# Attention and GELU MLP on one core: first batch's exps ahead of AV, gated loads, regrouped filler, q and k transposed in the idle score banks

## Chip, cores, metric

The kernel runs on one core of a Trainium2 chip. The time is the device time of one execution in microseconds (us), taken as the median of several runs; the span that the profile shows for the same execution is about 2 us shorter. Numbers that are read from a trace belong to one profiled execution.

## The reference

For 8 batches of 8 heads with 576 tokens of 64 elements, a causal attention with a decay from forget gates f, then a two-layer MLP with exact GELU over all 4608 tokens:

```python
scores = scale * np.matmul(q, k.transpose(0, 1, 3, 2))
cum    = np.cumsum(np.log(np.clip(f, 1e-4, 1.0)), axis=-1)
scores = np.where(causal, -1e9, scores + cum[..., :, None] - cum[..., None, :])
# ... softmax over the last axis ...
x = (attn @ v).transpose(0, 2, 1, 3).reshape(B * S, H * D)     # 4608 x 512
h = x @ w_in                                                   # 512 -> 2048
out = (0.5 * h * (1 + erf(h / np.sqrt(2)))) @ w_out            # 2048 -> 512
```

The decay's part in k goes into v as a weight per token (the weights wT, from f), the part in q cancels in the softmax.

## The kernel before

The program is a hand-ordered stream. For each batch: 16 score tiles (4 pairs of heads, 4 tiles each), the exps on ScalarE (ACT), causal masks on GpSimd (POOL), then AV (the product of the exps with the weighed v), the normalization and an output transpose. Then 16 blocks of GEMM1 with GELU. The 64 GEMM2 matmuls of batch b-1 are not run by themselves: they are filler, taken a few at a time between the score tiles of batch b. The 96-token transposes of the next batch's q and k stand between the GEMM1 blocks.

```python
    s_psum = ctx.enter_context(tc.tile_pool(name="s_psum", bufs=2, space=PSUM))  # scores
    o_psum = ctx.enter_context(tc.tile_pool(name="o_psum", bufs=2, space=PSUM))  # AV, transposes
    m_psum = ctx.enter_context(tc.tile_pool(name="m_psum", bufs=2, space=PSUM))  # GEMMs
# ... all loads are issued at once, in this order:
    # f; q, k of batch 0; v of batch 0; w_in; q, k, v of batch 1; w_out
# ...
    def transposes(b, i, which):            # one tensor (q or k) of one pair
        ps = o_psum.tile([P, 2, JT // 2, PT], BF16, tag="o", name="ps_t")
        # ... 6 transposes of 128 columns, then four VectorE copies of 64x288 ...
# ...
    for i in range(HP):                     # batch 0: everything transposed first
        transposes(0, i, 0)
        transposes(0, i, 1)
    # ... the weights wT ...
    for i in range(HP):
        weigh_v(0, i)                       # on GpSimd
    for b in range(B):
        # ... load_qk(b + 2), load_v(b + 2) ...
        for i in range(HP):
            for t in range(4):
                scores(b, i, t)             # exp and masks within
                # ... half a head of AV of pair i-1, normalize, to_xT ...
                take(fill, 2)               # two GEMM2 matmuls of batch b-1
        # ... take 4, AV, take 4, AV, take 8, to_xT ...
        for ffb in range(n_ff):
            gemm1(b, ffb)
            if b + 1 < B:
                if ffb % 2 == 1:
                    transposes(b + 1, ffb // 4, (ffb // 2) % 2)
                if ffb % 4 == 2:
                    weigh_v(b + 1, ffb // 4)
```

The softmax here doesn't subtract the row's maximum and nothing guards it: scores larger than these inputs give would overflow.

## Time and profile before

| | before |
|---|---|
| median of 3 runs | 420.17 us (418.93 to 422.03) |
| span of the profiled execution | 419.1 us |
| TensorE busy | 88% |
| first exp / first GEMM1 matmul | 23.7 / 57.8 us |
| batch 0's GEMM1, to the first score of batch 1 | 57.84 to 75.90: 18.1 us |
| period of a batch afterwards | 43.0, then 42.72 |

TensorE is the engine to feed. The list of waits (who waited for whom: total us, times, longest) of TensorE names what starves it; its first rows, and one further down:

```profile
PE s L210 <- ACT e L220: 10.3, 11, 1.2
PE o L241 <- POOL e L222: 9.7, 13, 7.2
...
PE o L241 <- POOL vw L201: 7.0, 1, 7.0
```

The last two belong to the start-up: one wait of 7.2 us for a mask and one of 7.0 us for the weighed v. The first is spread over the batches: 11 waits of at most 1.2 us in which a score tile waits for an exp to free its bank. The prediction below shows the other lines.

### The profile page before, as it was taken

How to read it: one execution, taken by the hardware profiler on the slowest of the kernel's cores; microseconds unless marked ns; L12 is line 12 of the kernel's file. 1: busy time of each engine (PE TensorE's matmuls, PEld its weight loads, DVE VectorE, ACT ScalarE, POOL GpSimd, SP SyncE). 2: the span in 40 equal slices, each digit the busy share in tenths (PEclk: the TensorE clock that was granted, in tenths of full speed). 3: DMA queues.
4: the chain of work that ended last, by engine and by line, in shares of the span. 5: the costliest groups of instructions: out<-in, count | busy, mean ns of one | idle time of the engine just before them, and what ended most of it. 6: DMA issues, size and time to landing. Idle time of an engine off the chain costs nothing.

```text
span 419.1 us, 7515 instructions
## 1 busy us (share of the span) xinstructions
PE 368.4 (88%) x3045; PEld 207.5 (50%) x3045; DVE 207.2 (49%) x466; ACT 215.0 (51%) x291; POOL 129.5 (31%) x262
## 2 busy tenths in 40 slices
PE   1340879899989998999899989998999999999996
PEld 1220645465546554655465546654664456444442
DVE  6930339534954486448634773468355924102001
ACT  3040736872677267725773577447743675350620
POOL 8408460446034603460247024700470042000000
PEclk9999969999999999999999999999999999999999
DMA  9999985801671166216521643100001000102002
GB/s 156 209 193 196 193 186 125 114 28 54 148 109 31 51 152 93 48 51 152 82 58 52 152 65 74 46 31 2 27 27 51 2 25 28 50 0 77 25 25 77
DMA packets 62738, 34.19 MB, mean 82 GB/s; under 512 B 43184, under 2 KB 57520, under 8 KB 62704
## 3 DMA queue, kind: packets, MB, share of 16 engines
q0 software_dynamic: 15328, 13.63, 20.9%
q1 hardware_dynamic: 47376, 20.08, 18.7%
q8 instruction: 24, 0.39, 0.4%
q14 instruction: 10, 0.08, 0.1%
HBM read 37.90 MB, written 9.44 MB: 113 GB/s over the span
## 4 chain that ended last, share of the span: by engine, by line
PE 77%; ACT 8%; POOL 5%; issue 4%; DVE 4%; ACTq 0%; POOLq 0%
PE ps L277 30%; PE ps L297 26%; PE s L210 7%; PE o L241 7%; ACT e L220 6%; PE ps_t L170 4%; POOL e L222 3%; PE ps_x L265 2%; DVE kT L181 2%; ACT L220 1%; DVE qB L181 1%; DVE qA L181 1%; POOL vw L195 1%; POOL q L98 1%; POOL k L98 1%
## 5 line engine op out<-in xcount | busy, mean ns | idle before, releaser
L289 ACT ACTIVATE g<-ps 128x512 bf16<-128x512 f32 x144 | 86.0, 597 | 125.7 <-PE ps L277 125.7
L297 PE MATMUL ps<-w_out_sb,g 128*128 128x512 bf16 x576 | 146.2, 379 | 0.0
L277 PE MATMUL ps<-xT_sb,w_in_sb 128*128 128x512 bf16 x576 | 136.5, 383 | 0.0
L220 ACT ACTIVATE e<-s 128x1024 bf16<-128x1024 f32 (+2 forms) x128 | 105.7, 862 | 56.2 <-PE s L210 47.6
L222 POOL TENSOR_SCALAR_AFFINE_SELECT e<-e 128x256 bf16<-128x256 bf16 x160 | 62.5, 406 | 114.7 <-ACT e L220 114.3
L277 PEld LDWEIGHTS <-w_in_sb 128*128 128x128 bf16 x576 | 54.0, 99 | 58.2 <-issue 3.5
L241 PE MATMUL o<-vw,e 128*128 128x65 bf16 x960 | 53.9, 196 | 17.7 <-POOL e L222 9.7
L297 PEld LDWEIGHTS <-g 128*128 128x128 bf16 x576 | 49.4, 98 | 37.8
L254 DVE RECIPROCAL r<-o 128x5 f32<-128x5 f32 x64 | 12.5, 195 | 110.5 <-PE o L241 110.5
L210 PE MATMUL s<-qA,kT 128*128 128x384 bf16 (+2 forms) x192 | 54.6, 289 | 11.3 <-ACT e L220 10.3
L181 DVE COPY kT<-ps_t 64x288 bf16<-64x288 bf16 x128 | 61.3, 479 | 2.5 <-PE ps_t L170 0.3
L306 DVE COPY ot<-ps 128x512 f32<-128x512 f32 x36 | 24.7, 687 | 75.7 <-PE ps L297 75.7
L210 PEld LDWEIGHTS <-kT 128*128 128x128 bf16 x384 | 37.2, 100 | 47.1 <-issue 17.2
L241 PEld LDWEIGHTS <-e 128*128 128x128 bf16 x960 | 45.5, 99 | 29.7 <-POOL e L222 11.3
L210 PE MATMUL s<-qB,kT 128*128 128x384 bf16 (+2 forms) x192 | 49.7, 290 | 0.0
L195 POOL TENSOR_TENSOR vw<-v,wT 128x640 bf16<-128x640 f32 x32 | 40.8, 1276 | 15.9 <-issue 13.1
L181 DVE COPY qA<-ps_t 64x288 bf16<-64x288 bf16 x64 | 30.6, 478 | 13.7 <-PE ps_t L170 12.5
L98 POOL DMA_DIRECT2D q<-in_q_dram x11 | 8.4, 766 | 80.3 <-PE ps_t L170 78.7
L255 DVE TENSOR_TENSOR x<-o,r 128x320 bf16<-128x320 f32 x64 | 31.4, 491 | 2.2
L181 DVE COPY qB<-ps_t 64x288 bf16<-64x288 bf16 x64 | 30.7, 480 | 0.9
L170 PE MATMUL ps_t<-ident_bf,q 96*128 96x96 bf16 x192 | 14.6, 216 | 11.6 <-POOL ident_bf masks.py:199 7.2
L170 PEld LDWEIGHTS <-q 96*128 96x128 bf16 x192 | 12.4, 103 | 18.9 <-issue 7.0
(33 smaller groups left out, 117.2 us busy)
## 6 DMA issues: line engine op xcount, KB each, us to landing
out_dram<-ot SPq DMA_DIRECT2D x36, 256.0 KB, 2.0
v<-in_v_dram SPq DMA_DIRECT2D x64, 128.0 KB, 3.1
q<-in_q_dram POOLq DMA_DIRECT2D x7, 576.0 KB, 6.0
k<-in_k_dram POOLq DMA_DIRECT2D x7, 576.0 KB, 8.0
w_in_sb<-in_moe_w_in_dram POOLq DMA_DIRECT2D x4, 512.0 KB, 12.1
v<-in_v_dram SPq DMA_DIRECT2D x8, 256.0 KB, 3.4
w_out_sb<-in_moe_w_out_dram POOLq DMA_DIRECT2D x4, 512.0 KB, 25.7
q<-in_q_dram POOLq DMA_DIRECT2D x4, 144.0 KB, 6.2
```

Of the source, the lines that this page charges most:

```text
L170: nc.tensor.transpose(ps[:, h, j, :], src[:, 2 * i + h, 2 * j * D : 2 * (j + 1) * D], ident_bf[:PT, :PT],)
L181: nc.vector.tensor_copy(rows[:, odd], ps[odd * D : (odd + 1) * D, h].rearrange("d j p -> d p j"),)
L195: nc.gpsimd.tensor_tensor(vw_of[b][:, hs, :, 0:D], v_of[b][:, hs, :, :], w.unsqueeze(3).to_broadcast([P, 2, NBLK, D]), Alu.mult,)
L210: nc.tensor.matmul(st[:, h, c : c + w], kT[i][:, K0[n] : K0[n] + P], qt[:, q0 : q0 + w], start=True, stop=True,)
L220: nc.scalar.activation(et[:, :, 0:c], st[:, :, 0:c], Act.Exp, scale=scale)
L222: nc.gpsimd.affine_select(out=et[:, :, c0 : c0 + P], in_=et[:, :, c0 : c0 + P], compare_op=Alu.is_ge, fill=0.0, base=0, pattern=[[0, 2], [ ...
L241: nc.tensor.matmul(o[:, m, :], e_of[b, i, t][:, h, c : c + P], vw_of[b][:, 2 * i + h, n, :], start=(n == 0), stop=(n == m),)
L255: nc.vector.tensor_tensor(x_of[b, i][:, :, h, :], o[:, :, 0:D], r.unsqueeze(2).to_broadcast([P, NBLK, D]), Alu.mult,)
L277: nc.tensor.matmul(ps, w_in_sb[:, kt, ffb * P : (ffb + 1) * P], xT_sb[:, kt, t0 : t0 + TC], start=(kt == 0), stop=(kt == n_dm - 1),)
L289: nc.scalar.activation(g_of[c][ffb], ps, Act.Gelu)
L297: nc.tensor.matmul(ps, g_of[c][kt][:, ts * P : (ts + 1) * P], w_out_sb[:, kt, :], start=(kt == 0), stop=(kt == n_ff - 1),)
L306: nc.vector.tensor_copy(ot, ps)
```

## The change

It has five parts.

1. *Load order.* q and k of batch 0 come in three portions. A GpSimd memset in v's tile holds v's loads back until q and k of four heads are issued (the "gate"). w_in comes in four column blocks, issued after the second pair's v is weighed; q, k of batch 1 and w_out only after batch 0's last exps are issued. q, k and v have one buffer each instead of two.
2. *Batch 0's transposes* write 64 rows each, so that one evacuation (the copy out of the bank) takes a whole tensor (kT) or half of one (qA, qB); two are on ACT.
3. *Batch 0's order.* Scores and exps begin after pair 0's transposes, and run two pairs ahead of AV; the tiles of exps have three buffers instead of two.
4. *Filler.* The GEMM2 matmuls are no longer two per tile: twelve follow the second score tile of a batch, and AV is put after the second to fourth tile. Batch 1 gets almost none before its last pair, because w_out comes late.
5. *Transposes of later batches* go into a score bank, q and k of a pair together, one group each four blocks; the eight copies follow. For batch 1 only three groups stand there, after blocks 8, 12 and 15; the fourth goes through the output banks within batch 1's own attention.

```diff
-    for i in range(HP):
-        load_qk(0, 2 * i, 2 * i + 2)
-    load_v(0)
+    load_qk_tokens(0, 0, 2)
     ... identities ...
+    load_qk_tokens(0, 2, 4)
+    v_of[0] = v_pool.tile([P, H, NBLK, D], FP32, tag="v", name="v0")
+    nc.gpsimd.memset(v_of[0][:, :, 0, 0:1], 0.0)
+    load_v(0, 0, 4)
+    load_qk_tokens(0, 4, 8)
+    load_v(0, 4, 8)
     ...
+    def transposes_pe(b, i, in_s=True):
+        if in_s:
+            both = s_psum.tile([P, 2, 2 * 512], BF16, tag="s", name="s_t")
+        ... both tensors' 12 transposes, then eight VectorE copies ...
     ...
+    def first_attention():
+        transposes(0); scores(0, 0, 0); scores(0, 0, 1)
+        ... wT; transposes(1); scores(0, 0, 2..3); transposes(2) ...
+        weigh_v(0, 0, nc.vector)
+        weigh_v(0, 1)
+        ... load_w_in(0..3); scores(0, 1, 0..3); transposes(3) ...
+        weigh_v(0, 2, nc.vector)
+        scores(0, 2, 0); scores(0, 2, 1)
+        attend_pair(0, 0)
+        ... and so on, two pairs ahead of AV ...
+    FILL = [[0, 12, 4, 4], [2, 3, 3, 2], [2, 3, 3, 2], [2, 2, 2, 2], [8, 4, 4, 0]]
+    FILL_1 = [[0, 0, 0, 0], [0, 0, 0, 0], [0, 0, 0, 0], [0, 0, 2, 4], [8, 4, 4, 0]]
     ...
-                take(fill, 2)
+                take(fill, counts[i][t])
     ...
-                if ffb % 2 == 1:
-                    transposes(b + 1, ffb // 4, (ffb // 2) % 2)
+                at = (8, 12, 15) if b == 0 else (1, 5, 9, 13)
+                if ffb in at:
+                    transposes_pe(b + 1, at.index(ffb))
```

(Several statements are put on one line here; the rest of the diff is the same code moved.)

More of the change, by code (lines that the diff above doesn't have):

```diff
@@ L75 @@
     consts = ctx.enter_context(tc.tile_pool(name="consts", bufs=1))
-    qk_pool = ctx.enter_context(tc.tile_pool(name="qk", bufs=2))
-    v_pool = ctx.enter_context(tc.tile_pool(name="v", bufs=2))
-    e_pool = ctx.enter_context(tc.tile_pool(name="e", bufs=2))
+    qk_pool = ctx.enter_context(tc.tile_pool(name="qk", bufs=1))
+    v_pool = ctx.enter_context(tc.tile_pool(name="v", bufs=1))
+    e_pool = ctx.enter_context(tc.tile_pool(name="e", bufs=3))
     x_pool = ctx.enter_context(tc.tile_pool(name="x", bufs=3))
@@ L87, with load_qk_tokens @@
     qk_of, v_of = {}, {}
-    def load_qk(b, h0=0, h1=H):
-        if b >= B:
-            return
+    def load_qk_tokens(b, h0=0, h1=H):
         if b not in qk_of:
-            qk_of[b] = (
-                qk_pool.tile([PT, H, JT * D], BF16, tag="q", name=f"q{b}"),
-                qk_pool.tile([PT, H, JT * D], BF16, tag="k", name=f"k{b}"),
-            )
+            qk_of[b] = [
+                qk_pool.tile([PT, H, JT * D], BF16, tag=n, name=f"{n}{b}")
+                for n in "qk"
+            ]
         for src, dst in zip((q, k), qk_of[b]):
@@ L107, in load_v @@
             v_of[b] = v_pool.tile([P, H, NBLK, D], FP32, tag="v", name=f"v{b}")
-        vt = v_of[b]
-        for h in range(h0, h1):
+        for n in range(NBLK):
             nc.sync.dma_start(
-                vt[:, h, 0:4, :],
-                v[b, h, 0:512].rearrange("(n p) d -> p n d", p=P),
-            )
-        nc.sync.dma_start(
-            vt[:, h0:h1, 4, :], v[b, h0:h1, 448:S].rearrange("h p d -> p h d")
-        )
+                v_of[b][:, h0:h1, n, :],
+                v[b, h0:h1, K0[n] : K0[n] + P].rearrange("h p d -> p h d"),
+            )
     f_sb = consts.tile([BH, S], FP32)
     nc.sync.dma_start(f_sb, f.rearrange("b h s -> (b h) s"))
-    for i in range(HP):
-        load_qk(0, 2 * i, 2 * i + 2)
-    load_v(0)
+    load_qk_tokens(0, 0, 2)
     ident_bf = consts.tile([P, P], BF16)
@@ L139, with load_w_in, load_w_out @@
     w_out_r = moe_w_out.rearrange("(ko ki) dm -> ki ko dm", ki=P)
-    for kt in range(n_dm):
-        nc.gpsimd.dma_start(w_in_sb[:, kt, :], w_in_r[:, kt, :])
-    load_qk(1)
-    load_v(1)
-    for kt in range(0, n_ff, 4):
-        nc.gpsimd.dma_start(w_out_sb[:, kt : kt + 4, :], w_out_r[:, kt : kt + 4, :])
+    def load_w_in(c):
+        f4 = slice(c * d_ff // 4, (c + 1) * d_ff // 4)
+        nc.gpsimd.dma_start(w_in_sb[:, :, f4], w_in_r[:, :, f4])
+    def load_w_out():
+        for kt in range(0, n_ff, 4):
+            nc.gpsimd.dma_start(w_out_sb[:, kt : kt + 4, :], w_out_r[:, kt : kt + 4, :])
     wT = consts.tile([P, NBLK, BH], FP32)
@@ L158, with transposes_first @@
     nc.scalar.activation(wk, cum, Act.Exp, bias=cum[:, S // 2 : S // 2 + 1], scale=-1.0)
-    psw = o_psum.tile([P, NBLK, BH], FP32, tag="o", name="psw")
     xT_sb = consts.tile([P, n_dm, N_tok], BF16)
-    def transposes(b, i, which):
-        src = qk_of[b][which]
-        ps = o_psum.tile([P, 2, JT // 2, PT], BF16, tag="o", name="ps_t")
+    def transposes_first(i, which):
+        src = qk_of[0][which]
+        ps = o_psum.tile([P, JT, PT], BF16, tag="o", name="ps_f")
         for h in range(2):
-            for j in range(JT // 2):
+            for j in range(JT):
@@ L170, in transposes, with evac @@
                 nc.tensor.transpose(
-                    ps[:, h, j, :],
-                    src[:, 2 * i + h, 2 * j * D : 2 * (j + 1) * D],
+                    ps[h * D : (h + 1) * D, j, :],
+                    src[:, 2 * i + h, j * D : (j + 1) * D],
                     ident_bf[:PT, :PT],
                 )
-        for h in range(2):
-            dst = (qA[i], qB[i])[h] if which == 0 else kT[i]
-            rows = dst[h * D : (h + 1) * D, :].rearrange(
-                "d (p j two) -> d two p j", j=JT // 2, two=2
-            )
-            for odd in range(2):
-                nc.vector.tensor_copy(
-                    rows[:, odd],
-                    ps[odd * D : (odd + 1) * D, h].rearrange("d j p -> d p j"),
-                )
+        def evac(eng, dst, r0, r1):
+            op = eng.copy if eng is nc.scalar else eng.tensor_copy
+            op(
+                dst[r0:r1, :].rearrange("d (p j) -> d p j", j=JT),
+                ps[r0:r1].rearrange("d j p -> d p j"),
+            )
@@ new lines, in transposes_first @@
+        if which:
+            evac(nc.vector, kT[i], 0, P)
+        else:
+            evac(nc.scalar if i < 2 else nc.vector, qA[i], 0, D)
+            evac(nc.vector, qB[i], D, P)
+    def transposes_pe(b, i, in_s=True):
+        shape = [P, 2, JT // 2, PT]
+        if in_s:
+            both = s_psum.tile([P, 2, 2 * 512], BF16, tag="s", name="s_t")
+            pss = [
+                both[:, w, 0:S].rearrange("p (h j t) -> p h j t", h=2, j=JT // 2)
+                for w in range(2)
+            ]
+        else:
+            pss = [
+                o_psum.tile(shape, BF16, tag="o", name="ps_t") for _ in range(2)
+            ]
+        for src, ps in zip(qk_of[b], pss):
+            for h in range(2):
+                for j in range(JT // 2):
+                    nc.tensor.transpose(
+                        ps[:, h, j, :],
+                        src[:, 2 * i + h, 2 * j * D : 2 * (j + 1) * D],
+                        ident_bf[:PT, :PT],
+                    )
+        for which, ps in enumerate(pss):
+            for h in range(2):
+                dst = (qA[i], qB[i])[h] if which == 0 else kT[i]
+                rows = dst[h * D : (h + 1) * D, :].rearrange(
+                    "d (p j two) -> d two p j", j=JT // 2, two=2
+                )
+                for odd in range(2):
+                    nc.vector.tensor_copy(
+                        rows[:, odd],
+                        ps[odd * D : (odd + 1) * D, h].rearrange("d j p -> d p j"),
+                    )
@@ L186, with weigh_v @@
     vw_of = {}
-    def weigh_v(b, i):
+    def weigh_v(b, i, eng=None):
         if b not in vw_of:
@@ L194, in weigh_v @@
         w = wT[:, :, bh : bh + 2].rearrange("p n h -> p h n")
-        nc.gpsimd.tensor_tensor(
+        eng = eng or nc.gpsimd
+        eng.tensor_tensor(
             vw_of[b][:, hs, :, 0:D],
@@ L200, in weigh_v @@
         )
-        nc.gpsimd.tensor_copy(vw_of[b][:, hs, :, D], w)
+        eng.tensor_copy(vw_of[b][:, hs, :, D], w)
     e_of = {}
@@ L315, in take, with attend_pair, load_next, transposes @@
                 return
-    for i in range(HP):
-        transposes(0, i, 0)
-        transposes(0, i, 1)
-    for n in range(NBLK):
-        nc.tensor.transpose(psw[:, n, :], wk[:, K0[n] : K0[n] + P], ident_fp[:BH, :BH])
-    nc.vector.tensor_copy(wT[:, 0:4, :], psw[:, 0:4, :])
-    nc.vector.tensor_copy(wT[D:P, 4, :], psw[D:P, 4, :])
-    for i in range(HP):
-        weigh_v(0, i)
-    for b in range(B):
-        fill = gemm2(b - 1) if b else iter(())
-        load_qk(b + 2)
-        load_v(b + 2)
+    def attend_pair(b, i):
+        for h in range(2):
+            attend(b, i, h, (4, 3, 2, 1, 0))
+            normalize(b, i, h)
+    def first_attention():
+        def load_next():
+            load_qk_tokens(1, 0, 4)
+            load_qk_tokens(1, 4, 8)
+            load_w_out()
+        def transposes(i):
+            transposes_first(i, 1)
+            transposes_first(i, 0)
+        transposes(0)
+        scores(0, 0, 0)
+        scores(0, 0, 1)
+        psw = o_psum.tile([P, NBLK, BH], FP32, tag="o", name="psw")
+        for n in range(NBLK):
+            nc.tensor.transpose(
+                psw[:, n, :], wk[:, K0[n] : K0[n] + P], ident_fp[:BH, :BH]
+            )
+        nc.vector.tensor_copy(wT[:, 0:4, :], psw[:, 0:4, :])
+        nc.vector.tensor_copy(wT[D:P, 4, :], psw[D:P, 4, :])
+        transposes(1)
+        scores(0, 0, 2)
+        scores(0, 0, 3)
+        transposes(2)
+        weigh_v(0, 0, nc.vector)
+        weigh_v(0, 1)
+        for c in range(4):
+            load_w_in(c)
+        for t in range(4):
+            scores(0, 1, t)
+        transposes(3)
+        weigh_v(0, 2, nc.vector)
+        scores(0, 2, 0)
+        scores(0, 2, 1)
+        attend_pair(0, 0)
+        scores(0, 2, 2)
+        scores(0, 2, 3)
+        weigh_v(0, 3)
+        to_xT(0, 0)
+        scores(0, 3, 0)
+        scores(0, 3, 1)
+        attend_pair(0, 1)
+        scores(0, 3, 2)
+        scores(0, 3, 3)
+        load_next()
+        to_xT(0, 1)
+        attend_pair(0, 2)
+        to_xT(0, 2)
+        attend_pair(0, 3)
+        to_xT(0, 3)
+    FILL = [[0, 12, 4, 4], [2, 3, 3, 2], [2, 3, 3, 2], [2, 2, 2, 2], [8, 4, 4, 0]]
+    FILL_1 = [[0, 0, 0, 0], [0, 0, 0, 0], [0, 0, 0, 0], [0, 0, 2, 4], [8, 4, 4, 0]]
+    def attention(b, fill, counts):
         for i in range(HP):
@@ L334 @@
                 scores(b, i, t)
-                if i:
-                    if t == 0:
-                        attend(b, i - 1, 0, (4, 3))
-                    elif t == 1:
-                        attend(b, i - 1, 0, (2, 1, 0))
-                        normalize(b, i - 1, 0)
-                    elif t == 2:
-                        attend(b, i - 1, 1, (4, 3))
-                    else:
-                        attend(b, i - 1, 1, (2, 1, 0))
-                        normalize(b, i - 1, 1)
-                if i >= 2 and t == 1:
-                    to_xT(b, i - 2)
-                take(fill, 2)
+                if i >= 2 and t == 0:
+                    to_xT(b, i - 2)
+                if i and t == 1:
+                    attend(b, i - 1, 0, (4, 3))
+                elif i and t == 2:
+                    attend(b, i - 1, 0, (2, 1, 0))
+                    normalize(b, i - 1, 0)
+                elif i and t == 3:
+                    attend(b, i - 1, 1, (4, 3, 2, 1, 0))
+                    normalize(b, i - 1, 1)
+                if b == 1 and i == 0 and t == 2:
+                    transposes_pe(1, 3, in_s=False)
+                    load_qk_tokens(2)
+                take(fill, counts[i][t])
         i = HP - 1
-        take(fill, 4)
+        take(fill, counts[HP][0])
         attend(b, i, 0, (4, 3, 2, 1, 0))
@@ L353 @@
         to_xT(b, i - 1)
-        take(fill, 4)
+        take(fill, counts[HP][1])
         attend(b, i, 1, (4, 3, 2, 1, 0))
         normalize(b, i, 1)
-        take(fill, 8)
+        take(fill, counts[HP][2])
         to_xT(b, i)
         take(fill, 999)
+    for b in range(B):
+        if b == 0:
+            first_attention()
+            load_v(1)
+        else:
+            load_v(b + 1)
+            attention(b, gemm2(b - 1), FILL_1 if b == 1 else FILL)
         for ffb in range(n_ff):
@@ L362 @@
             if b + 1 < B:
-                if ffb % 2 == 1:
-                    transposes(b + 1, ffb // 4, (ffb // 2) % 2)
+                at = (8, 12, 15) if b == 0 else (1, 5, 9, 13)
+                if ffb in at:
+                    transposes_pe(b + 1, at.index(ffb))
                 if ffb % 4 == 2:
                     weigh_v(b + 1, ffb // 4)
+        if 0 < b < B - 2:
+            load_qk_tokens(b + 2)
     take(gemm2(B - 1), 999)
```

## The prediction

> **What bounds the kernel now.** I read the page first (busy shares, then the slices), then the chain of waits in time order, then TensorE's timeline at the batch borders, then who waited for whom.
>
> The busy shares say that TensorE is the engine to feed (88% of the span), and the slices say where it is not fed:
>
> ```profile
> PE 368.4 (88%) x3045; PEld 207.5 (50%) x3045; DVE 207.2 (49%) x466; ACT 215.0 (51%) x291; POOL 129.5 (31%) x262
> ...
> PE   1340879899989998999899989998999999999996
> ...
> GB/s 156 209 193 196 193 186 125 114 28 54 148 109 31 51 152 93 48 51 152 82 58 52 152 65 74 46 31 2 27 27 51 2 25 28 50 0 77 25 25 77
> ```
>
> One slice is 10.5 us. In slices 1 to 4 TensorE is at 1, 3, 4 and 0 tenths while the DMA moves about 190 GB/s; after slice 5 it is nearly full. So there are two parts: a start-up of 58 us, and a steady state.
>
> The start-up by the chain of waits (start, length, what; "issue" is time in which the profile shows no releaser):
>
> ```profile
> 7.24 0.65 PE ps_t L170 x6
> ...
> 23.25 0.48 DVE kT L181
> 23.77 0.42 DVE wT L323
> 24.21 0.24 DVE wT L324
> 24.45 8.94 issue
> ...
> 34.84 1.21 POOL vw L195
> ...
> 38.96 0.75 POOL q L98
> 39.71 0.76 POOL k L98
> 40.48 1.84 POOL e L222 x5
> ...
> 57.33 0.72 PE ps_x L265 x5
> 58.04 3.41 PE ps L277 x8
> ```
>
> From 7 to 24 us all four pairs of q and k are transposed and evacuated by 32 VectorE copies of 0.48 us, before the first scores. From 24.4 to 33.4 GpSimd waits for v (its tile's loads land 2.7/9.1/25.0 us after issue, minimum/median/maximum): they were issued from 1.4 us on, but shared the DMA with w_in, w_out and the next batch. Then come four weighings of v, two DMA issues and the masks; AV starts in earnest at 42.4, the first GEMM1 matmul at 57.8.
>
> The steady state by TensorE's timeline at a batch border:
>
> ```profile
> 118.90 0.33 PE L210 MATMUL s<-qA,kT 128*128 128x384 bf16 x1
> ...
> 120.15 0.59 PE L297 MATMUL ps<-w_out_sb,g 128*128 128x512 bf16 x2
> 121.97 0.30 PE L210 MATMUL s<-qA,kT 128*128 128x320 bf16 x1 [1.23 <-ACT e L220]
> ...
> 161.62 0.33 PE L210 MATMUL s<-qA,kT 128*128 128x384 bf16 x1
> ```
>
> The same first score stands at 118.90 and 161.62: a batch is 42.72 us. Of its 26.76 us of attention (118.90 to GEMM1's start at 145.66) I count by start-to-start times: 4 x 1.415 scores, 4 x 0.96 AV, 4 x 0.27 output transposes, 64 GEMM2 matmuls of 0.2155: 24.4. So 2.37 us per batch is lost, 1.39 of it at one spot, where the third score tile waits for ACT's table load and first exp.
>
> **What the Trainium skill says.** (1) "TensorE: Matmul & The Clock Gate", Part 1: TensorE's clock is halved until it has been busy for a window of some 3.4 us, and again after idleness. The trace agrees in kind: the 384-column scores at 22.59 start 0.30 us apart, at 45.92 0.17, and the first GEMM1 matmuls at 58 us 0.43 apart against 0.216. (2) "DMA: Bandwidth & Descriptors", Issuing engines are not separate DMA queues: transfers of all engines interleave on the same 16 DMA engines. The trace agrees: a v load issued at 8.3 us by SyncE lands 25 us later among GpSimd's weight loads. (3) "VectorE: DVE Perf Modes", Why PSUM operands drop a tier: a PSUM source gets at most two elements per cycle, one if fp32. The trace agrees: 128x576 contiguous bf16 takes 0.45 us, 64x288 strided 0.48. (4) "ScalarE: Activation LUTs", What ACT_TABLE_LOAD costs: about 1.28 us; the trace has 1.28.
>
> **The change, part by part.**
>
> *Load order.* A GpSimd memset in v's tile, after the first four heads of q and k are issued, holds v's loads back until about 5.4 us; w_in is issued only after v is weighed, w_out and batch 1 at the end of batch 0's exps. q, k, v of batch 0 and f are 1.18 + 1.31 + 0.15 = 2.64 MB as written; at the slices' 195 GB/s 13.5 us, from 2.7 on: all landed by about 16 instead of 33. That removes the 9 us of waiting. New: w_in cannot start before GpSimd has masked pair 0 (exp end about 17.5) and weighed one pair (1.5): issue at about 20 to 22, 2.1 MB more = 11 us, landed in four column blocks from 24 to 34. GEMM1 needs one block per 3.5 us. Then batch 1's q and k (1.18) with v (1.31): about 45; w_out about 57.
>
> *Transposes of batch 0.* Per pair, three evacuations of 576 elements (my estimate 0.78 us, the 0.18 fixed plus 0.3 per 288 of the 0.48 row) instead of eight of 0.48: 9.4 us for batch 0, not 15.7, two of them on ACT, and scores begin after pair 0, not pair 3. k and q of pair 0 land at about 6; transposes (12 cold, 0.08 each) to 8.4, qA on ACT to 9.3, qB to 10.1 (it waits for ACT: they read one bank), scores, first exp at about 11.3 instead of 23.67.
>
> *Exps ahead of AV.* In the trace four exps of a pair take 3.67 us when ACT is fed (46.64 to 50.31): 14.7 for 16, plus two copies of about 0.7: 16. Unhindered the last would end at 27.5; TensorE at half clock (all the start-up's work would be 29 us cold, 15 warm) and the VectorE copies between pairs hold it up: about 32. After the last exp the kernel before needs 4.6 us to GEMM1 (53.2 to 57.8) with one pair of AV left; here two pairs are left: 4.6 plus about 1.5 to 2. GEMM1 starts at about **38 instead of 57.8: -20** (34 if warm, 42 if cold).
>
> *GEMM1 of batch 0.* 13.84, plus 1.04 for two of its three groups of transposes, plus about 1.3 for a cold start: its 16th block ends at 54.2, against 75.9: **-21.7**.
>
> *Batch 1 gives back.* Its attention has almost no GEMM2 filler (w_out is late), 6 of 64 matmuls before its last pair is done. So ACT bounds it. The score tiles also wait for VectorE: pair 1's transposes stand 3 blocks (2.6 us) before the end, its eight copies 8 x 0.49 = 3.93 end 1.55 after the end; pair 2's copies 5.5 after it, and the third score tile takes that bank. First exp at +3.6, pair 0 done at +7.7, three pairs of 3.67: +18.8. Then the rest of AV and 52 fillers, 14.2, and GEMM1 15.8: 48.8 against 43.0: **+5.8**.
>
> *Batches 2 to 7.* Transposes now use the score banks. The last group stands after block 13; its copies take 3.93 + 0.2, while TensorE reaches the second score tile of the next batch, which by the built program's semaphores waits for exactly these copies, after two blocks (1.73) and one score tile (0.44): a new stall of about **2.0 us**. The old wait on ACT (2.37 with its companions) goes, since 12 fillers follow the second tile. Two output transposes come 0.87 us after an AV whose normalization needs about 1.0: 2 x 0.13. At the end only four fillers cover the last normalization, and the last GEMM2 copy (0.68) stands before the xT copy: about 0.5. Lost: 2.8 against 2.37: **+0.4 per batch, +2.4 in all**. The tail (two chunks of GEMM) stays.
>
> Sum: -21.7 + 5.8 + 2.4 = **-13.5**. 420.2 - 13.5 = 406.7; I say **406**.
>
> **The rivals.**
> 1. *The steady state gains too* (the idle score banks remove a wait): the copies end in time, 2.3 us x 6 = 14 more: about 392. Against it: in the trace the transposes of the kernel before cost TensorE no wait at all in the steady state (pairs of blocks with six transposes are 1.99 us apart = 1.73 + 0.26), so there is nothing for this part to gain, and the semaphore is plain.
> 2. *w_in or batch 1's loads become the bound*: GpSimd is in order, so w_in stands behind masks that stand behind exps, and the DMA idles from about 16 to 21. If first exps slip by 5 us, so do w_in, GEMM1 and q, k of batch 1 (needed at its ninth block): about 412. For it: one long chain of engines; against it: some 4 us of slack for each.
> 3. *TensorE goes cold in batch 1*, whose filler-less attention leaves it half idle: a cold pair is 2.8 + 1.9 = 4.7 us, over ACT's 3.67: +1 per pair, about 410.
> 4. *All start-up work runs warm* and ACT alone bounds it: GEMM1 at 34: about 402.
>
> **Range and chances.** Start-up ±4, batch 1 ±2.5, steady state ±0.4 x 6: added in squares about 5.3, and 1.28 sigma of that is 7: 399 to 413. Faster by over 2% means below 411.8, about one sigma above the forecast: 0.82. Within 2%: 0.16. Slower needs batch 1 and the start-up both to fail: 0.02.
>
> **What would show it.** In the changed kernel's profile: first exp at 11 to 12 us; no wait for v over 2 us; first GEMM1 matmul at 34 to 42; in the waits, second scores of batches 2 to 7 waiting about 2 us each for VectorE copies of kT, and about 43.1 us between the same first scores of successive batches; in batch 1 about 49. I am wrong if the steady period falls below 42 (rival 1), if GEMM1 waits for w_in or the transposes for q (rival 2), or if scores in batch 1 start 0.30 apart (rival 3).

## The result, and the profile after

The changed kernel takes **402.79 us** (median of 4 runs, 402.03 to 403.86) against 420.03 us for the kernel before in the same rounds. The ratio is **0.9586**, 95% interval 0.954 to 0.9632.

The page of the changed kernel: TensorE's busy row and its 40 slices of now 10.0 us.

```profile
PE 365.4 (91%) x3044; PEld 207.0 (52%) x3093; DVE 203.3 (51%) x448; ACT 217.5 (54%) x293; POOL 128.8 (32%) x259
...
PE   2998968999899989998999899998999899999995
```

The hole in the first four slices (1, 3, 4 and 0 before) is gone; what is left of the start-up is the 2 in the first slice. The 6 in the sixth slice (50 to 60 us) is the beginning of batch 1. After that an 8 comes about every four slices, that is once per batch.

*The start-up*, by the chain of waits (start, length, what):

```profile
5.88 8.92 DMA k<-in_k_dram
...
14.84 1.34 PE ps_f L170 x24
...
24.75 1.03 ACT e L257
...
28.43 0.32 PE s L247 x2
...
33.62 0.45 PE ps_x L302 x5
...
34.13 7.78 PE ps L314 x35
```

GEMM1 begins at 34.13 instead of 57.84. The chain starts with a transfer: the k of heads 4 to 7 is issued at 5.88 and has landed at 14.8 (TensorE had waited 0.42 us for it). Then transposes, scores and exps alternate. The last exp ends at 29.7, and 4.4 us later the last output transposes are through. ACT's timeline has the first exp at 10.01; of the 19.7 us from there to the last exp's end, ACT is busy for 13.5.

The clock of TensorE is read from the distance of two matmuls of one size. In the changed kernel's timeline (start, busy, engine, line, what), two pairs of 384-column scores:

```profile
20.79 0.50 PE L247 MATMUL s<-qA,kT 128*128 128x384 bf16 x1
21.09 0.53 PE L247 MATMUL s<-qB,kT 128*128 128x384 bf16 x1
...
25.83 0.32 PE L247 MATMUL s<-qA,kT 128*128 128x384 bf16 x1 [0.16 <-ACT e L257]
25.99 0.32 PE L247 MATMUL s<-qB,kT 128*128 128x384 bf16 x1
```

At 21 us they start 0.30 us apart, at 26 us 0.16: TensorE ran at half rate ("cold") for the first two thirds of the start-up and at full rate ("warm") from about 24 on. So GEMM1 of batch 0 starts warm: 34.13 to 48.81 for its 16 blocks with two groups of transposes, 14.7 us.

*Batch 1*, in the same timeline:

```profile
50.41 0.34 PE L247 MATMUL s<-qA,kT 128*128 128x384 bf16 x1 [0.92 <-DVE kT L217]
...
53.49 0.35 PE L247 MATMUL s<-qA,kT 128*128 128x448 bf16 x1 [2.47 <-ACT e L257]
...
54.36 0.30 PE L247 MATMUL s<-qA,kT 128*128 128x320 bf16 x1 [0.33 <-DVE kT L217]
...
56.13 0.48 PE L247 MATMUL s<-qA,kT 128*128 128x384 bf16 x1
56.40 0.52 PE L247 MATMUL s<-qB,kT 128*128 128x384 bf16 x1
```

The first score is at 50.41 instead of 75.90. The first three score tiles wait 0.92 us (for VectorE's copies), 2.47 (for ACT: a table load of 1.28 us and the first exp) and 0.33. The missing filler is not the reason for the first two waits: filler stands only after the second tile, and with it, in batch1_fill and o_fill below, they are still 0.92 and 2.47. What batch 1 lacks is the filler that follows the second tile elsewhere: 62 of its 64 GEMM2 matmuls stand behind the last scores. After these gaps the same scores start 0.27 us apart, so TensorE has fallen back to half rate (the granted clock of 50.4 to 67 is 0.90), as it does with the filler too. This batch takes 48.64 us, in the kernel before 43.0.

*Batches 2 to 7.* The border between batches 1 and 2, and the first score of batch 3:

```profile
99.05 0.33 PE L247 MATMUL s<-qA,kT 128*128 128x384 bf16 x1
...
101.50 0.36 PE L247 MATMUL s<-qA,kT 128*128 128x448 bf16 x1 [1.85 <-DVE kT L217]
...
101.89 2.75 PE L334 MATMUL ps<-w_out_sb,g 128*128 128x512 bf16 x12
...
141.95 0.33 PE L247 MATMUL s<-qA,kT 128*128 128x384 bf16 x1
```

The second score tile waits 1.85 us for VectorE's copies out of its bank, and the twelve GEMM2 matmuls that could have covered it stand behind it. A period is 141.95 - 99.05 = 42.90, before 42.72. The waits of TensorE over the whole span say the same; their order has turned round:

```profile
PE s L247 <- DVE kT L217: 12.3, 8, 1.9
PE ps_f L170 <- DMA k<-in_k_dram: 5.9, 2, 5.5
```

The biggest entry is a wait that the kernel before did not have. The waits for masks and for v that led before are gone.

| stage, from the two profiled executions | before | after | difference |
|---|---|---|---|
| start to GEMM1 | 57.84 | 34.13 | -23.7 |
| GEMM1 of batch 0, to the end of its 16th block | 18.1 | 14.7 | -3.4 |
| from there to the first score of batch 2 | 43.0 | 50.2 | +7.2 |
| batches 2 to 7 and the tail | 300.2 | 301.05 | +0.85 |
| span | 419.1 | 400.1 | -19.0 |

(The profiled execution of the kernel before was 1 us slower than its median, that of the changed kernel 0.7 us faster; by medians the difference is 17.2.)

### The profile page after: what moved, and what is told of

The parts are those of the page before. It is cut to its first block, busy times and chain, and to the rows that moved or that the text cites. A ratio compares the mean times of both kernels' runs of the same rounds, so it can differ in the third digit from the quotient of the medians.

```text
span 400.1 us, 7526 instructions
## 1 busy us (share of the span) xinstructions
PE 365.4 (91%) x3044; PEld 207.0 (52%) x3093; DVE 203.3 (51%) x448; ACT 217.5 (54%) x293; POOL 128.8 (32%) x259
## 4 chain that ended last, share of the span: by engine, by line
PE 80%; DVE 10%; issue 3%; ACT 2%; DMA 2%; POOL 2%; POOLq 0%; ACTq 0%
PE ps L334 31%; PE ps L314 26%; PE s L247 11%; PE o L278 7%; DVE kT L217 4%; PE s_t L205 3%; PE ps_x L302 2%; DMA k<-in_k_dram 2%; ACT e L257 2%; DVE qA L217 2%; DVE qB L217 1%; DVE ot L343 1%; DVE xT_sb L305 1%; PE ps_f L170 1%; POOL q L97 1%
## 5 line engine op out<-in xcount | busy, mean ns | idle before, releaser
L334 PE MATMUL ps<-w_out_sb,g 128*128 128x512 bf16 x543 | 136.4, 379 | 1.7
L314 PE MATMUL ps<-xT_sb,w_in_sb 128*128 128x512 bf16 x560 | 130.2, 379 | 1.4
L247 PE MATMUL s<-qA,kT 128*128 128x384 bf16 (+2 forms) x192 | 55.4, 297 | 18.3 <-DVE kT L217 12.3
L217 DVE COPY kT<-s_t 64x288 bf16<-64x288 bf16 x108 | 51.7, 479 | 1.5
L232 POOL TENSOR_TENSOR vw<-v,wT 128x640 bf16<-128x640 f32 x30 | 38.3, 1277 | 31.9 <-PE o L278 22.1
L278 PEld LDWEIGHTS <-e 128*128 128x128 bf16 x960 | 41.4, 99 | 9.3 <-DVE x L292 1.1
L278 PE MATMUL o<-vw,e 128*128 128x65 bf16 x960 | 44.9, 195 | 0.9 <-POOL e L259 0.7
L217 DVE COPY qA<-s_t 64x288 bf16<-64x288 bf16 x54 | 25.8, 479 | 19.8 <-PE s_t L205 18.7
L217 DVE COPY qB<-s_t 64x288 bf16<-64x288 bf16 x54 | 25.9, 481 | 0.7
L305 DVE COPY xT_sb<-ps_x 128x576 bf16<-128x576 bf16 x32 | 14.5, 453 | 10.4 <-PE ps_x L302 10.4
L302 PE MATMUL ps_x<-ident_bf,x 128*128 128x128 bf16 x160 | 14.4, 221 | 2.0 <-DVE x L292 2.0
## 6 DMA issues: line engine op xcount, KB each, us to landing
w_out_sb<-in_moe_w_out_dram POOLq DMA_DIRECT2D x4, 512.0 KB, 16.2
```

The source lines that it names most:

```text
L217: nc.vector.tensor_copy(rows[:, odd], ps[odd * D : (odd + 1) * D, h].rearrange("d j p -> d p j"),)
L232: eng.tensor_tensor(vw_of[b][:, hs, :, 0:D], v_of[b][:, hs, :, :], w.unsqueeze(3).to_broadcast([P, 2, NBLK, D]), Alu.mult,)
L247: nc.tensor.matmul(st[:, h, c : c + w], kT[i][:, K0[n] : K0[n] + P], qt[:, q0 : q0 + w], start=True, stop=True,)
L278: nc.tensor.matmul(o[:, m, :], e_of[b, i, t][:, h, c : c + P], vw_of[b][:, 2 * i + h, n, :], start=(n == 0), stop=(n == m),)
L302: nc.tensor.transpose(ps[:, K0[m] : K0[m] + P], x_of[b, i][:, m, :, :], ident_bf)
L314: nc.tensor.matmul(ps, w_in_sb[:, kt, ffb * P : (ffb + 1) * P], xT_sb[:, kt, t0 : t0 + TC], start=(kt == 0), stop=(kt == n_dm - 1),)
```

## The experiments

The theory after reading the result: the start-up gives what is gained; the score-bank transposes and the filler schedule nearly cancel each other in the steady state; batch 1 gives some back for want of filler. The rivals: the steady state is at its floor anyway; the load order alone makes the start-up; batch 1 is bound by its loads. Ten kernels ran, all correct, with 4 timed runs each.

| run | median, us | ratio to before (95%) | GEMM1 starts | batch 1 | later period |
|---|---|---|---|---|---|
| before | 420.0 to 420.4 | 1 | 57.8 | 43.0 | 42.72 |
| changed kernel | 402.79 | 0.9586 (0.954-0.9632) | 34.1 | 48.6 | 42.89 |
| o_banks | 391.02 | 0.932 (0.9275-0.9364) | 32.7 | 54.2 | 40.89 |
| fill_first | 392.64 | 0.9349 (0.9316-0.9383) | 35.0 | 49.1 | 41.17 |
| before_fill | 405.69 | 0.9649 (0.9627-0.9671) | 57.8 | 40.9 | 40.89 |
| loads_only | 412.93 | 0.9823 (0.9801-0.9845) | 49.5 | 43.0 | 42.73 |
| compute_only | 414.92 | 0.9869 (0.9848-0.989) | 47.1 | 48.9 | 42.89 |
| ungated | 404.69 | 0.9642 (0.9597-0.9688) | 35.7 | 48.9 | 42.89 |
| one_behind | 405.99 | 0.9655 (0.9632-0.9678) | 36.9 | 49.1 | 42.89 |
| batch1_fill | 401.1 | 0.9557 (0.9528-0.9587) | 32.9 | 46.0 | 42.89 |
| o_fill | **385.8** | 0.9192 (0.9147-0.9237) | 33.9 | 45.8 | 40.71 |
| w_out_late | 387.39 | 0.9228 (0.9184-0.9272) | 33.5 | 47.0 | 40.71 |

The last three columns are read from the profiled execution; "batch 1" is from its first score to the first score of batch 2. One caution about the column of GEMM1: the changed kernel, o_banks, fill_first, batch1_fill, o_fill and w_out_late have the same start-up up to GEMM1, and their first exps all come at 10.0, yet GEMM1 starts anywhere from 32.7 to 35.0. By the distances of their scores, TensorE gets to full rate between 16.3 us (o_banks) and 24.2 us (the changed kernel), and in fill_first it falls back once, from 25.8 to about 29. So a difference of about 2 us in this column between two single executions shows nothing by itself.

### The steady state: transposes against filler

**o_banks**: the changed kernel, but from batch 2 on the transposes go through the output banks as before, one tensor every two blocks.

```diff
-                at = (8, 12, 15) if b == 0 else (1, 5, 9, 13)
+                at = (8, 12, 15) if b == 0 else ()
+                if b and ffb % 2 == 1:
+                    transposes_o(b + 1, ffb // 4, (ffb // 2) % 2)
```

> The changed kernel with the transposes of batches 2 to 7 as before: through the two o banks, one tensor every two blocks, each evacuated before the next; batch 0 and the transposes for batch 1 as changed, filler schedule as changed. Theory (score banks for the transposes cost 1.86 us per batch and save nothing, since the old way never made TensorE wait): period about 41.0, about 392. Rival (the idle banks take a wait away, the fillers hide the rest): 403 or more.

Measured: 391.02 us. The period falls from 42.89 to 40.89: the score-bank transposes cost 2.0 us in each of six batches, 1.86 of it the wait shown above. That is the whole 11.8 us between this kernel and the changed one. In the profiled execution (394.39, the slowest of the four) batch 1 took 54.2. Two lines show why, a row of TensorE's waits and a row of GpSimd's timeline:

```profile
PE o L299 <- POOL e L280: 4.6, 1, 4.6
```

```profile
52.45 1.28 POOL L253 TENSOR_TENSOR vw<-v,wT 128x640 bf16<-128x640 f32 x1 [17.60 <-DMA v<-in_v_dram]
```

GpSimd works in order. It waited until 52.45 for batch 1's v, which was loading beside w_out, then made four weighings, and only then the masks; AV waited 4.6 us for one of them, and TensorE was at half rate until about 67 us (two equal scores at 64.12 and 64.42 are 0.30 apart). So batch 1 has a second weakness besides the missing filler, and it varies between executions.

**fill_first**: the changed kernel with eight of the twelve filler matmuls moved to before the second score tile.

```diff
-    FILL = [[0, 12, 4, 4], ...
+    FILL = [[8, 4, 4, 4], ...
```

> The changed kernel with 8 of the 12 GEMM2 fillers of a batch's start moved from behind the second score tile to behind the first (batches 2 to 7). Theory (a new wait for the score bank: TensorE stands 1.86 us before the second score tile until pair 3's eight copies out of that bank are done): 8 x 0.2155 = 1.72 us of work lies in that hole, so the batch period falls from 42.90 to about 41.1, six times: 402.8 - 10.5 = about 392, and the wait of the score for the kT copy falls below 0.3 us. Rival (the hole is really the table load and first exp of ACT, and the fillers only shift it to the third tile): about 402, with a wait of the third tile on ACT.

Measured: 392.64 us, period 41.17. TensorE's waits no longer have the 12.3 us for VectorE, one of 0.9 in batch 1 is left. Eight matmuls of 0.216 us are 1.73, nearly the length of the stall: work that was there all along covers it. This tells the wait's nature: VectorE was not too slow for the batch, TensorE merely arrived at the bank too early.

**before_fill**: the kernel before with the changed filler schedule and AV order, nothing else.

```diff
-                take(fill, 2)
+                take(fill, counts[i][t])
     (counts as FILL; AV after tiles 1, 2, 3 instead of 0, 1, 2, 3)
```

> The kernel before with the changed filler schedule and AV order alone (0, 12, 4, 4 behind the first four score tiles and so on). Theory (the old 2.37 us lost per batch were the wait of the third score tile for ACT, which 12 fillers behind the second tile cover): period 42.73 to about 41.0, seven batches with GEMM2 fillers: 420 - 11 = about 409. Rival (the filler schedule is worth nothing without the score banks): 418 to 420.

Measured: 405.69 us, 3 less than expected. The period is 40.89 from batch 1 on, 1.83 under that of the kernel before, and GEMM1 of batch 0 took 16.0 us rather than 18.1: in the kernel before its first eight matmuls start 0.43 us apart, here 0.22. Whether the new AV order or chance kept TensorE warm was not separated. So this one rearrangement, without a new load order and without any new buffer, alone makes the kernel 14.4 us faster (420.12 in its rounds, less 405.69), where the whole change makes it 17.2 faster. What the other parts gain at the start is nearly all lost again, to the score-bank transposes (2.0 us in each of six batches) and in batch 1 (40.9 us here, 48.6 in the changed kernel).

### The start-up: loads against computation

**loads_only**: the computation of the kernel before with the changed order of the loads.

```diff
-    load_qk(0, ...) ; load_v(0) ; w_in ; load_qk(1) ; load_v(1) ; w_out
+    load_qk(0, 0, 2) ; load_qk(0, 2, 4) ; (gate) ; load_v(0, 0, 4) ; load_qk(0, 4, 8) ; load_v(0, 4, 8)
+    (w_in after two weighings; batch 1 and w_out after batch 0's attention)
```

> The kernel before with the changed order of loads alone: v held back behind the first four heads of q and k, w_in behind the first two weighings, batch 1 and w_out after batch 0's attention. Theory (the start-up is two chains, v's landing and the order of computation, and each alone hides the other): v is there by about 15, but the 32 copies still end at 24; then weighings 6, w_in issues 3, masks 2, and 15 us to GEMM1: first GEMM1 matmul at about 51 instead of 57.8, total about 413. Rival (the load order is the whole gain): GEMM1 at about 38, total about 400.

Measured: 412.93 us, as expected, with GEMM1 at 49.5, 1.5 us sooner than I had thought.

**compute_only**: the changed computation with the old order of the loads (q, k, v double-buffered as before, so that they can be issued early).

```diff
-    load_qk_tokens(0, 0, 2) ; load_qk_tokens(0, 2, 4) ; (gate) ; load_v(0, 0, 4) ; ...
+    load_qk_tokens(0, 2 * i, 2 * i + 2) for four i ; load_v(0)
+    (then at once: w_in ; load_qk_tokens(1) ; load_v(1) ; load_w_out())
```

> The changed kernel with the old order of loads: all of q and k, v ungated, w_in, batch 1, w_out straight away (q, k and v buffers doubled again for that). Theory (as before): exps of pairs 0 and 1 run early, but the weighing of v on VectorE stands in front of pair 3's copies and v lands at about 33 again; in the changed kernel the way from that weighing to GEMM1 is 16 us, so GEMM1 at about 49 instead of 34.1, total about 418. Rival (running the exps ahead is the whole gain): GEMM1 below 40, total below 408.

Measured: 414.92 us, GEMM1 at 47.1. Here the exps run early, the first at 11.4, but batch 0's v lands only at about 31: VectorE waits 12.2 us for it before a weighing, GpSimd 8.6, and one AV stands 10.8 us behind VectorE. The 3 us under the expectation are partly the 2 us by which GEMM1 starts earlier; the rest was not traced. Taken alone the loads move GEMM1 by 8.3 us and the computation by 10.7, together by 23.7, which is 4.7 more than the sum. Each alone uncovers the other as the bound: behind early exps AV waits for v, and an early v waits for the exps. Of the computation only the place of AV was tried by itself (one_behind); the 64-row transposes, the early scores and the third buffer of exps were not separated.

**ungated**: the changed kernel without the memset that holds v back.

```diff
-    nc.gpsimd.memset(v_of[0][:, :, 0, 0:1], 0.0)
```

> The changed kernel without the memset that holds v's loads back; w_in stays late. Theory (q and k of pairs 2 and 3 are what the start-up waits for: k's last heads land at 14.8 us and TensorE waits for them): v's 256-byte rows now share the DMA with q and k from 1.4 us on, so k's last heads land 1 to 3 us later and GEMM1 starts that much later: 404 to 406. Rival (the gate does nothing, holding w_in back is what matters): 402.5 to 403.5.

Measured: 404.69 us, 1.9 more than the changed kernel, though the intervals of the ratios overlap. In its profiled execution the k of the first pair lands 2.2 us later (TensorE's first transpose at 7.72 instead of 5.51), the first exp comes at 11.3 instead of 10.0, and GEMM1 starts at 35.7 instead of 34.1. The first two are clear: in every profiled execution with the gate and this start-up the first exp comes at 10.0. But it is not what I expected: the k of the last heads lands at 14.97, only 0.2 us later, and TensorE does not wait for it. The 35.7 lies just outside the 32.7 to 35.0 of the equal start-ups, and here too TensorE falls back to half rate for a while (26.5 to 29.4). So the gate brings the first exp 1.3 us forward; a gain in the whole time, 1.9 us by the medians, is likely but not shown.

**one_behind**: batch 0 with AV one pair behind the exps instead of two.

```diff
         scores(0, 1, 0); scores(0, 1, 1)
+        attend_pair(0, 0)
         ...
-        scores(0, 2, 0); scores(0, 2, 1)
-        attend_pair(0, 0)
+        scores(0, 2, 0); scores(0, 2, 1)
+        attend_pair(0, 1)
```

> The changed kernel with batch 0's AV one pair behind the exps instead of two (AV of pair 0 within pair 1's scores). Theory (with v landed by 15 us, the running ahead is no longer what counts; copies, DMA and TensorE's clock set the pace): GEMM1 within 1.5 us of 34.1, 402 to 404.5. Rival (running ahead is needed to hide masks and weighings): GEMM1 3 us or more later, 406 or more.

Measured: 405.99 us, GEMM1 at 36.9. My expectation was wrong here, and the rival came nearer, just short of its own limits of 3 us and 406: GEMM1 starts 2.7 us later, outside the 32.7 to 35.0 of the equal start-ups. A row of TensorE's timeline and one of ACT's:

```profile
19.40 1.83 PE L278 MATMUL o<-vw,e 128*128 128x65 bf16 x30 [1.60 <-DVE vw L238]
```

```profile
22.13 1.41 ACT L257 ACTIVATE e<-s 128x1024 bf16<-128x1024 f32 x2 [3.20 <-PE s L247]
```

AV of pair 0 waits 1.6 us for the weighed v. TensorE works in order, so the next scores wait behind it, and ACT sits idle for 3.2 us. The last exp ends at 33.9 instead of 29.7. On top of it GEMM1 starts cold: its first 36 matmuls take 8.9 us, at 0.216 each they would be 7.8. TensorE also stays at half rate until about 28.7, in the changed kernel until 24.2; how much of the loss is the order itself and how much this clock was not separated. An operation with a late operand should not stand ahead of the work that feeds another engine.

### Batch 1

**batch1_fill**: the changed kernel with the same filler in batch 1 as in the others.

```diff
-            attention(b, gemm2(b - 1), FILL_1 if b == 1 else FILL)
+            attention(b, gemm2(b - 1), FILL)
```

> The changed kernel with the ordinary filler schedule in batch 1 too. Theory (batch 1 takes 50.2 us because its attention has hardly any filler, though w_out has landed between 46.5 and 54.1, before it is used): period of batch 1 about 45, total about 398. Rival (w_out comes too late, or the fillers delay the exps that bound this stretch): 402 to 405, with a wait for w_out or longer gaps on ACT.

Measured: 401.1 us; its interval overlaps the changed kernel's, so a gain by itself is not shown. The four runs lie between 398.29 and 402.74. In the fastest, the profiled one, batch 1 took 46.0 instead of 48.6; another 1.3 us of its lead are an earlier GEMM1 in a start-up that was not changed. TensorE did not wait for w_out. The spread goes with TensorE's mean granted clock: 0.996 in the run of 398.29, 0.986 in that of 402.74. The changed kernel has the same pattern: 0.994 and 0.995 in the runs of 402.0 and 402.1, 0.986 and 0.987 in those of 403.5 and 403.9. Where in these slower, unprofiled runs TensorE went to half rate, no trace shows; in the profiled executions it was the start-up and batch 1.

### Putting it together

**o_fill**: o_banks, the filler in batch 1, and the last two filler matmuls of a batch after its last output transpose.

```diff
 (o_banks, and)
-    FILL = [[0, 12, 4, 4], ..., [8, 4, 4, 0]]
+    FILL = [[0, 12, 4, 4], ..., [6, 4, 4, 0]]
-            attention(b, gemm2(b - 1), FILL_1 if b == 1 else FILL)
+            attention(b, gemm2(b - 1), FILL)
```

> Both removable losses taken out at once: from batch 2 on the transposes go through the output banks again, batch 1 has the same GEMM2 filler as the other batches, and the last output transposes stand before the last two filler matmuls. My theory, that the score-bank transposes cost 2.0 us in each of six batches and the missing filler 2 to 4 us in batch 1, adds them up: 391.0 less 2 to 4 less some 0.2 a batch: about 387, period at most 40.9, batch 1 about 46. Rival: batch 1 is bound by when v and w_out of the loads arrive (in the profiled run of the output-bank kernel TensorE waited 4.6 us for masks that stood on GpSimd behind weighings that waited for v until 52.4): then the filler only waits in its turn and the time stays at 390 to 391, batch 1 at 50 or more.

Measured: **385.8 us** (385.17 to 388.24), 8% under the kernel before and 4% under the changed one (its rounds ran on another chip, where the kernel before took 420.43). TensorE's 40 slices (of 9.6 us), and the batch border:

```profile
PE   2978969999999999999999999999999999999995
```

```profile
137.34 0.35 PE L268 MATMUL s<-qA,kT 128*128 128x448 bf16 x1
137.53 0.35 PE L268 MATMUL s<-qB,kT 128*128 128x448 bf16 x1
137.72 2.75 PE L355 MATMUL ps<-w_out_sb,g 128*128 128x512 bf16 x12
```

From the seventh slice on (58 us) no dent is left before the tail. The second score tile and the filler follow without a wait (there is no bracket). The period is 40.71.

**w_out_late**: o_fill, but w_out is issued only after the first weighing of batch 1's v.

```diff
-            load_w_out()                       (after load_qk_tokens(1, 4, 8))
+                    if b == 0 and ffb == 2:
+                        load_w_out()           (after weigh_v(1, 0))
```

> As the run before, but w_out is issued only after the first weighing of batch 1's v, so that v no longer shares the DMA with it. If batch 1's v is what makes the masks late, GpSimd's wait for v ends at about 41 to 43 instead of 45 to 52, TensorE waits for no mask in batch 1, and the time falls another 1 to 3 us: about 385, with less spread between runs. Rival: w_out then lands at 52 to 57, the filler of batch 1 waits for it right after the second score tile, and batch 1 loses as much as it gains: 387 to 390.

Measured: 387.39 us: no gain (the intervals overlap), and batch 1 takes 47.0 instead of 45.8. The time is the rival's; its reason is not. The first twelve filler matmuls of batch 1 and the score after them in w_out_late, then the same in o_fill, with the second score tile before them:

```profile
53.83 5.33 PE L355 MATMUL ps<-w_out_sb,g 128*128 128x512 bf16 x12
58.95 0.35 PE L268 MATMUL s<-qA,kT 128*128 128x320 bf16 x1
```

```profile
53.45 0.35 PE L268 MATMUL s<-qA,kT 128*128 128x448 bf16 x1 [2.47 <-ACT e L278]
...
53.83 4.44 PE L355 MATMUL ps<-w_out_sb,g 128*128 128x512 bf16 x12
58.10 0.30 PE L268 MATMUL s<-qA,kT 128*128 128x320 bf16 x1
```

In both they are far over the 2.75 us that the twelve take at full rate, and it is the clock alone. In the trace's single records all twelve start 0.427 us apart in w_out_late; in o_fill eight do (the first of them 0.38), the last four 0.22 to 0.26. There is no gap in which they wait for w_out, though it lands late (its four parts at 50.5, 53.9, 56.7 and 60.0; the thirteenth matmul waits about 0.1 us for the last). So the weighing of v did start at 43.4, and TensorE waited for no mask; but it waited for none in o_fill's profiled execution either, so there was nothing to win. And TensorE stood at half rate longer: the granted clock of 49 to 66 us is 0.80, in o_fill 0.90. Whether the late w_out or chance made it so stays open.

## Why the prediction was right

The forecast was 406 us, in a range of 399 to 413, with a chance of 0.82 for faster by over 2%; measured 402.79. The mechanism held in each step, but not all of its details did; the sum of -13.5 became -19.0 in the two profiled executions because of these terms.

1. *Load order.* v was named as the wait to go, and in batch 0 it went. For batch 1's v GpSimd waits 9.7 us, against the sign "no wait for v over 2 us"; TensorE's longest wait for a mask is 0.7 us, so here it costs little. w_in was expected to be issued at 20 to 22 and was issued at 17.5; GEMM1 did not wait for it (rival 2 did not come). Not foreseen: the k of heads 4 to 7 lands at 14.8 and TensorE waits for it, though only 0.42 us.
2. *Transposes of batch 0.* "12 cold, 0.08 each", 1.92 us for a pair's 24, was too much (and 6 plus 1.92 is 7.9, where the prediction has 8.4). The chain shows 24 in 1.34 us, and the first exp came at 10.0 instead of 11.3. The evacuations were 0.72 to 0.76 us on VectorE and 0.62 on ACT, for an estimate of 0.78.
3. *Exps ahead of AV: -20.* It was -23.7. Of the 3.9 us between 38 and 34.1, the earlier first exp is 1.3, the exps themselves 1.0 (19.7 us from first to last instead of 20.7), and 1.6 is what follows the last exp (4.4 us, not 6). This is the mis-sized term with the largest weight. The number of rival 4 came true (GEMM1 at 34), its reason did not: until about 24 us TensorE was cold, and ACT was idle for 6.2 of the 19.7 us.
4. *GEMM1 of batch 0.* The term "about 1.3 for a cold start" was wrong: TensorE had been warm for 10 us. GEMM1 took 14.7 instead of 16.2. Steps 3 and 4 together are -27.1 instead of -21.7.
5. *Batch 1: +5.8.* It was +7.2. Its GEMM1 started 34.3 us after batch 0's last block (48.81 to 83.1); the prediction has 48.8 - 15.8 = 33.0 (in which 52 fillers are counted, though 64 less 6 is 58). Rival 3 came in part, and its sign of being wrong nearly showed: the pair of scores at 56.1 started 0.27 us apart, for the 0.30 that was named. Half rate lasted there for about 3 us, not for the whole attention.
6. *Batches 2 to 7: +2.4.* It was about +0.85. The stall was forecast at 2.0 us and measured at 1.86, at the tile, bank and copies named. o_banks gave 2.0 per batch when it was taken away. The gain from the filler, forecast as 2.37 less some 0.8 of new small losses, was 1.83 (before_fill). Two terms that nearly cancel were each sized within 0.3 us.

Rival 1, "the steady state gains too", at about 392 us, did not happen in the changed kernel. But its number was right for a kernel whose copies don't stand in the way: o_banks took 391.02 and fill_first 392.64. The prediction's reason against it, that the transposes through the output banks cost TensorE nothing, held: before_fill and o_banks, with those, have the shortest period of all but o_fill and w_out_late, which use them too.

## What to carry to other kernels

A buffer that is idle while a stage runs is not idle at the stage's border: ask which instruction takes it next, and put independent matmuls between the last reader and that one. Where two parts of a change act on the same stretch, run each part alone: here a regrouped filler that wins 1.8 us a batch stood beside transposes that lose 2.0, and the sum of the two hid both. Before a small shift in one execution is read as an effect, look how far executions of the same stretch differ: here 2.2 us. An operation in an in-order stream whose operand comes late belongs after the work that feeds the next engine.

## What the Trainium skill lacked or had wrong

- "TensorE: Matmul & The Clock Gate", Part 1, puts the fall to half rate after an idle window of about 3.4 us. In batch 1 of the changed kernel the longest gap was 2.47 us, with 0.92 and 0.33 us beside it, and the 384-column scores afterwards were 0.27 us apart instead of 0.16. So no single gap of that length is needed here. The page's section "A second HAM failure mode" does say that frequent short idling can make the clock swing, but has no figure for how much idling. The page also says that recorded clock events can be unreliable, but not how that looks: in the changed kernel the granted clock reads 1.00 from 16 to 24 us, where the same scores start 0.30 us apart. The distance of equal matmuls is the safer reading.
- "TensorEngine Tiling (Array Packing)", Theoretical Speedup, gives up to 2 times where a dimension is at most 64. In the changed kernel's start-up 24 transposes of 96x64 took 1.27 us cold (19.52 to 20.79, where the next scores start), 0.053 us each; six of 96x128, cold, took 0.48 us (55.15 to 55.63), 0.080 each. That is 1.5 times per transpose, and since a 96x64 one moves half as much, no gain per element. The page has no figure for transposes.
